# Moving VectorE's attention pieces, one lower half and one scaling in a fused attention and gated MLP kernel

## The chip, the cores and the metric

The kernel runs on one core of a Trainium2 chip. The metric is the device time in microseconds; lower is better. The kernel before takes 954.05 us (median of three runs, 953.96 to 954.59).

## What is computed

The reference is a linear attention without softmax, a root-mean-square norm over each head, and a two-layer MLP whose gate is h * erf(softplus(h)):

```python
kv = np.einsum('bhsd,bhse->bhde', k, v)
out = np.einsum('bhsd,bhde->bhse', q, kv)
rms = np.sqrt(np.mean(out * out, axis=-1, keepdims=True) + 1e-06)
x = (out / rms * g_norm)            # 8 batches, 8 heads, 576 rows, 64 columns
x = x.transpose(0, 2, 1, 3).reshape(4608, 512)
h = x @ w_in                        # 512 x 2048
sp = np.maximum(h, 0.0) + np.log1p(np.exp(-np.abs(h)))
return (h * erf(sp)) @ w_out        # 2048 x 512
```

The two weight matrices arrive in double precision, as pairs of 32-bit words; the rest is single precision.

## The kernel before

The 4608 rows are cut into nine groups T of 512 rows. Groups 0 to 7 hold 512 of the 576 rows of one batch each; group 8 collects the 64 rows left over ("tails") of all eight. The hidden width of 2048 is cut into 16 slices f of 128.

**Exact products from three forms.** From group 1 on, the products are made from rounded parts: a value x is split into an upper part (ScalarE, `upper`, L588), a lower part x - upper (VectorE, `lower_only`, L591) and a combination of both (VectorE, `both_only`, L594). One product (`product`, L642) is twelve matmuls of 512 columns: eight into `n_ps` (upper and lower forms) and four into `m_ps` (combined form). ScalarE scales `n_ps` out of PSUM (L1034, L899), VectorE adds `m_ps` (`add`, L628).

**Preparing the weights.** A 64-bit word pair becomes one single-precision number in `w_split` and `w_join`. `w_split` runs on ScalarE: it scales the upper word into `w_e` (L220) and converts the lower word into `w_m` (L221). `w_join` runs on VectorE: a shift (L230), the sign bit (L233) and an addition (L240). Eighteen pieces are converted, four of 512 columns and fourteen of 1024. `w_order` and `due` set when: `weights` splits one piece ahead of the one it joins. Four pieces are split in the prelude, the others in or after step 0. In step group 1 the weights are also split into their three forms, `w_upper` on ScalarE (L612) and `w_lower` on VectorE (L615, L618), and stored in DRAM, from which they are fetched again for each later group.

**Steps n = 0 to 31** handle groups 0 and 1, one slice f per step. A step makes h of one slice (L884, or `hidden` L650), its softplus, and the projection of the slice of five steps earlier (`project`, L706). Every four steps ScalarE applies Erf (L919). `steps[f]` holds three lists of attention pieces: the first is run at the step's start (behind up to two `w_lower`), the second behind the softplus, the third behind the projection. `pieces_of` fills them.

**Batches m = 8 to 36** handle groups 2 to 8 with four slices each (b = 0 to 3 in a group). A batch has four units i: a hidden product into PSUM, ScalarE's scaled copy, VectorE's add, ScalarE's softplus (L1049). Then ScalarE applies Erf (L1053), VectorE multiplies h by it (L1076) to give g, and four results j follow: the product of g's forms of the previous batch with `w_out`, each added into `e` by two VectorE instructions (L969 or L623, and L628). g of the previous batch is cut in two halves, `cut_upper` (ScalarE) in unit 0 and `cut_lower` (VectorE) for half 0 in unit 0 and for half 1 in unit 1. Results 0 and 1 read half 0, results 2 and 3 read half 1.

**The attention of the next group** is threaded through the batches, one pair p of heads per batch, as pieces run at `places`: 0, 2, 3, 5, 6 and 8 (the last batch of a group: 7). Place i + 1 is behind unit i, place 5 + j behind result j. In groups 3 to 7 the "visit" (L439) at place 2 makes, on TensorE, the attention output of pair p (L446, L454) and already the turned q and the kv product of the next pair (L466). Behind it ScalarE squares the output (L472), and `turned` copies the turned q (ScalarE, L338) and, for even pairs, the tails (VectorE, L345). At place 3 VectorE halves the square into two parts (`halve`, L500, L501), keeps the tail's output (`keep_tail`, L477) and reduces kv (`kv_kept`, L354, L361). Place 5 is the mean (L516, L517) with Ln, Exp and a square on ScalarE (L531 to L533), with activation tables loaded around them; place 6 is norm on VectorE (L539, L542, L551); place 8 cuts x into three forms. The next group's first hidden product needs those forms of all four pairs.

In groups 1 and 2 `prepare` (L366) makes the turned q and kv of its own pair, a step ahead of the visit, and calls `turned` and `kv_kept`.

**Queues.** Each engine works its instructions off in the order in which this code writes them; PSUM has six banks in rotation for the products (`banks`, three pairs) and one two-bank tile `at_ps` for the visit.

Of the kernel before, what the change touches and what calls it, by code (L numbers as in the profile page):

```python
# [39 lines left out]
FP32 = mybir.dt.float32  # L40
# [3 lines left out]
AF = mybir.ActivationFunctionType  # L44
ALU = mybir.AluOpType
# [5 lines left out]
BATCH = 4  # L51
# [3 lines left out]
FIRST = 2  # L55
# [5 lines left out]
def kernel(  # L61
# [10 lines left out]
    nc = tc.nc  # L72
# [6 lines left out]
    NP = H // 2  # L79
# [67 lines left out]
    def load_last(T, p):  # L147
        if T < B:
            nc.sync.dma_start(
                out=q_last[p % 2 * R : p % 2 * R + R, p // 2],  # L150
                in_=q[T, 2 * p : 2 * p + 2, G:S, :].rearrange("h r d -> r h d"),
            )

    g_col = const.tile([P, 1], FP32, name="g_col")
    for i in range(2):
        nc.gpsimd.dma_start(
            out=g_col[i * D : i * D + D, :], in_=g_norm.rearrange("(d one) -> d one", one=1)
# [29 lines left out]
    w_raw, w_cv = {}, {}  # L187
# [17 lines left out]
    def words(which, f):  # L205

        raw = w_raw[which, f]
        hi, lo = (
            raw.bitcast(kind).rearrange("p (n two) -> p n two", two=2)[:, :, half]
            for kind, half in ((FP32, 1), (U32, 0))  # L210
        )
        return hi, lo, raw.rearrange("p (n two) -> p n two", two=2)[:, :, 1]

    def w_split(which, f, k):


        hi, lo, _ = words(which, f)
        e = early.tile([P, G * k], I32, name="w_e", tag="w_e", bufs=2)
        m = early.tile([P, G * k], I32, name="w_m", tag="w_m", bufs=2)
        nc.scalar.activation(e.bitcast(FP32), hi, AF.Copy, scale=2.0**-112)  # L220
        nc.scalar.activation(m, lo, AF.Copy, scale=2.0**-29)  # L221
        w_cv[which, f] = e, m

    def w_join(which, f, k):


        hi = words(which, f)[2]
        e, m = w_cv.pop((which, f))
        w_raw.pop((which, f))
        nc.vector.tensor_scalar(  # L230
            out=e, in0=e, scalar1=3, scalar2=None, op0=ALU.logical_shift_left
        )
        nc.vector.scalar_tensor_tensor(  # L233
            out=e, in0=hi, scalar=-(1 << 31), in1=e, op0=ALU.bitwise_and, op1=ALU.bitwise_or
        )
        if which == "in":
            out_ = w_in_sb[:, f : f + k].rearrange("p t c f -> p (t c f)")
        else:
            out_ = w_out_sb[:, f : f + k, :].rearrange("p t f -> p (t f)")
        nc.vector.tensor_tensor(out=out_.bitcast(I32), in0=e, in1=m, op=ALU.add)  # L240
# [5 lines left out]
        + [(min(f + LAG, (f + FC) // 2 + 1), "out", f, 2) for f in range(0, FC, 2)]  # L246
    )
    w_at = {"load": 0, "split": 0, "join": 0}

    def w_next(what):  # L250
        i = w_at[what]
# [29 lines left out]
    def halves_of(t):  # L281
        return t.rearrange("p (a t) -> p a t", a=2)
# [50 lines left out]
    def turned(T, p, ps):  # L333

        qT = attp.tile([P, G], FP32, name="qT", tag="qT")
        if isinstance(ps, tuple):
            for a in range(2):
                nc.scalar.copy(halves_of(qT)[:, a], ps[a][:, 0 : 2 * P])  # L338
        else:
            nc.scalar.copy(halves_of(qT), ps[:, :, 0 : 2 * P])  # L340
        if p % 2 == 0:
            tails[T] = attp.tile([P, 2, R], FP32, name="qT_last", tag="t")
            for a in range(2):
                t = ps[a] if isinstance(ps, tuple) else ps[:, a]
                nc.vector.tensor_copy(out=tails[T][:, a], in_=t[:, 2 * P : 2 * P + R])  # L345
        if p == NP - 2:
            for i in range(NP):
                load_last(T + 1, i)
        ready[T, p] = qT, tails[T][:, p % 2]

    def kv_kept(T, p, at):

        kv = kv_of(T, p)
        nc.vector.tensor_reduce(  # L354
            out=kv[:, 0:D],
            in_=at[:, :, kv_cols].rearrange("p a e -> p e a"),
            op=ALU.add,
            axis=mybir.AxisListType.X,
        )
        for i in range(2):  # L360
            nc.vector.tensor_copy(out=kv[rows_of[1 - i], D : 2 * D], in_=kv[rows_of[i], 0:D])  # L361
# [4 lines left out]
    def prepare(T, p):  # L366

        at = at_tile()
        for product_ in turn_products(T, p, (at[:, 0], at[:, 1])):
            product_()  # L370
        for product_ in kv_products(T, p, at, crossed=False):
            product_()
        turned(T, p, at)
        kv_kept(T, p, at)

    def attention(T, p, pools=None):

# [5 lines left out]
        then = divmod(T * NP + p + 1, NP)  # L383
# [55 lines left out]
        def visit():  # L439


            qT, tail = ready.pop((T, p))
            at = st["at"] = at_tile()
            x = halves_of(qT)
            for a, i, o in ((0, 0, 0), (0, 1, 1), (1, 0, 1), (1, 1, 0)):
                nc.tensor.matmul(  # L446
                    at[rows_of[o], a, 0 : 2 * P],
                    lhsT=bd[rows_of[i], a * D : a * D + D],
                    rhs=x[rows_of[i], a],
                    start=True,  # L450
                    stop=True,
                )
            for s in rows_of:
                nc.tensor.matmul(  # L454
                    at[s, 0, 2 * P : 2 * P + R], lhsT=bd[s, 0:D], rhs=tail[s], start=True, stop=True
                )
            st["o"] = at[:, :, 0 : 2 * P]
            st["next"] = fused and then[0] < B
            if st["next"]:
                ps = pair_of_banks("q0_ps", "q1_ps")  # L460
                kvs = list(kv_products(*then, at, crossed=True))
                turns = list(turn_products(*then, ps))
                while kvs or turns:
                    for some in (turns, kvs):
                        for product_ in some[:4]:
                            product_()  # L466
                        del some[:4]
            if fused:
                st["sq"] = x_new.tile([P, G], FP32, name="sq", tag="x")
            else:  # L470
                st["sq"] = qT
            nc.scalar.activation(two(st["sq"]), st["o"], AF.Square)  # L472
            if st["next"]:
                turned(*then, ps)

        def keep_tail():
            nc.vector.tensor_copy(  # L477
# [96 lines left out]

        prepare_ = partial(prepare, T, p)
        if fused:
            first_ = (prepare_,) if (T, p) == (FIRST + 1, 0) else ()
            pieces = (first_, (visit,), (halve, keep_tail, loads))
        elif halves:
            pieces = ((prepare_,), (visit,), (halve, keep_tail, loads))  # L580
        else:
            pieces = ((prepare_, loads), (visit,), (keep_tail,))
# [187 lines left out]
            w_next(what)  # L770


    first_batch, batches = FIRST * NB, NG * NB
    w_seq = {
        which: [(which, f) for _ in range(NG - FIRST) for f in range(FC)] for which in ("in", "out")
# [15 lines left out]
    def pieces_of(T):  # L791


        steps = [([], [], []) for _ in range(FC)]
        for p in range(NP):
            products, apply, halve, mean, norm, split = attention(T, p)
            f = (BATCH - 1) * (p + 1) if T < FIRST else BATCH * p

            steps[f][2 if T == FIRST or p == 1 else 1].append(products)
            steps[f + 1][1].append(apply)  # L800
            steps[f + 2][0].append(halve)
            with_erf = (f + 2) % BATCH == BATCH - 1

            place = 2 if T < FIRST and p == 0 else 1
            steps[f + 2][place].append(partial(mean, table=not with_erf))
            steps[f + 3][0].append(norm)
            steps[min(f + 4, FC - 1)][0].append(split)
        return steps
# [27 lines left out]
    for n in range(FIRST * FC + 1):  # L836
        T, f = divmod(n, FC)
# [9 lines left out]
        if T < FIRST:  # L847
            if f == 0:
                steps = pieces_of(T + 1)
# [105 lines left out]
    def cut_lower(h, half, t):  # L955
        lower(part(h, half), *(t[:, i] for i in range(3)))
# [27 lines left out]
    for m in range(first_batch, batches + 1):  # L984
# [25 lines left out]
        def pieces(place):  # L1010
            while todo and places[-len(todo)] <= place:
                todo.pop(0)()
# [15 lines left out]
        for i in range(BATCH):  # L1028
            if m < batches:
                n_ps, m_ps = hidden(T, b * BATCH + i)  # L1030
            fetch(i)

            def evacuate():
                nc.scalar.activation(h[:, i], n_ps, AF.Copy, scale=SHIFT - 1.0)  # L1034
                add(h[:, i], m_ps)


            early_copy = i == 0 and m == B * NB
            if early_copy:
                evacuate()  # L1040
            if i == 0:
                for half in range(done, 2):
                    g.append(cut_upper(old_h, half))
            if done <= i < 2:
                cut_lower(old_h, i, g[i])
            if m < batches:
                if not early_copy:
                    evacuate()
                nc.scalar.activation(s[:, i], h[:, i], AF.Softplus)  # L1049
            pieces(i + 1)  # L1050
        if m < batches:
            for i in range(2):
# [29 lines left out]
        old_h = h  # L1082
# [33 lines left out]
```

## Time and profile before

| | us |
|---|---|
| device time, median of three | 954.05 |
| span of the profiled execution | 952.8 |
| TensorE busy (matmuls) | 924.1 |
| VectorE busy | 720.2 |
| ScalarE busy | 617.2 |
| first steady batch starts (hidden product of m = 8) | 255.8 |
| visits of group 5 (L446), starts | 564.25, 588.50, 612.90, 637.15 |
| norm of the same batches (L539), starts | 581.04, 606.15, 631.26, 656.36 |

In the profile's lines, DVE is VectorE, ACT is ScalarE, PE is TensorE's matmuls and PEld its weight loads. A timeline line gives the start in the execution, the duration, the engine, the line of the code, the instruction, what it writes and reads, how often, and in brackets the idle time of the engine just before it with what ended it. Matmuls are pipelined, so a matmul's listed duration is longer than the distance to the next one.

### The profile page before, as it was taken

How to read it: one execution, taken by the hardware profiler on the slowest of the kernel's cores; microseconds unless marked ns; L12 is line 12 of the kernel's file. 1: busy time of each engine (PE TensorE's matmuls, PEld its weight loads, DVE VectorE, ACT ScalarE, POOL GpSimd, SP SyncE). 2: the span in 40 equal slices, each digit the busy share in tenths (PEclk: the TensorE clock that was granted, in tenths of full speed). 3: DMA queues.
4: the chain of work that ended last, by engine and by line, in shares of the span. 5: the costliest groups of instructions: out<-in, count | busy, mean ns of one | idle time of the engine just before them, and what ended most of it. 6: DMA issues, size and time to landing. Idle time of an engine off the chain costs nothing.

```text
span 952.8 us, 15391 instructions
## 1 busy us (share of the span) xinstructions
PE 924.1 (97%) x5998; PEld 685.8 (72%) x5998; DVE 720.2 (76%) x1060; ACT 617.2 (65%) x844; POOL 2.4 (0%) x10
## 2 busy tenths in 40 slices
PE   6999999999999999999999999999999999999998
PEld 4444445656687877887788878886888788888886
DVE  2777648887677787888688878888787877788667
ACT  3999876776766666666656666666666666665552
POOL 1000000000000000000000000000000000000000
PEclk9999999999999999999999999999999999999999
DMA  9866406888789898899689978987887668777872
GB/s 255 290 191 207 140 1 232 320 351 313 233 304 338 327 336 303 298 340 322 203 285 327 312 268 315 325 300 252 271 320 260 256 240 346 283 272 300 346 272 61
DMA packets 108271, 259.99 MB, mean 273 GB/s; under 512 B 43992, under 2 KB 66856, under 8 KB 108200
## 3 DMA queue, kind: packets, MB, share of 16 engines
q1 hardware_dynamic: 106488, 256.73, 76.2%
q10 hardware_dynamic: 1648, 2.29, 0.8%
q8 instruction: 47, 0.77, 0.3%
q14 instruction: 24, 0.20, 0.1%
q0 software_dynamic: 64, 0.00, 0.0%
HBM read 224.40 MB, written 34.60 MB: 272 GB/s over the span
## 4 chain that ended last, share of the span: by engine, by line
PE 65%; DVE 15%; ACT 11%; DMA 4%; issue 3%; SPq 0%; DVEq 0%; ACTq 0%
PE n_ps L650 31%; PE m_ps L650 16%; PE o_ps L706 9%; PE h_ps L884 4%; DVE h L628 3%; ACT s L1053 2%; DVE g_forms L591 2%; DVE e L628 2%; DMA w_raw<-in_moe_w_in_dram 1%; ACT L105 1%; ACT L1053 1%; DMA w_in_parts<-w_in 1%; PE at_ps L446 1%; DVE x L551 1%; DVE u L542 1%
## 5 line engine op out<-in xcount | busy, mean ns | idle before, releaser
L650 PE MATMUL n_ps<-x_forms,w_in_parts 128*128 128x512 f32 x896 | 229.8, 397 | 9.0 <-DVE x_forms L591 4.2
L650 PE MATMUL n_ps<-w_out_parts,g_forms 128*128 128x512 f32 x928 | 232.5, 392 | 0.9 <-DVE qT_last L345 0.9
L1049 ACT ACTIVATE s<-h 128x512 f32<-128x512 f32 x112 | 70.8, 633 | 209.7 <-DVE h L628 209.7
L650 PEld LDWEIGHTS n_ps<-x_forms,w_in_parts 128*128 128x128 f32 x896 | 168.2, 190 | 49.1 <-ACT x_forms L588 6.0
L650 PEld LDWEIGHTS n_ps<-w_out_parts,g_forms 128*128 128x128 f32 x928 | 172.5, 188 | 39.3 <-DVE qT_last L345 2.2
L650 PE MATMUL m_ps<-w_out_parts,g_forms 128*128 128x512 f32 (+1 forms) x468 | 124.3, 388 | 0.0
L650 PE MATMUL m_ps<-x_forms,w_in_parts 128*128 128x512 f32 x448 | 120.8, 392 | 0.0
L628 DVE TENSOR_TENSOR h<-m_ps,h 128x512 f32<-128x512 f32 x116 | 79.7, 687 | 52.4 <-ACT h L1034 34.9
L706 PE MATMUL o_ps<-w_out_sb,h_sb 128*128 128x512 f32 x224 | 101.7, 597 | 0.2 <-DVE h_sb L834 0.2
L650 PEld LDWEIGHTS m_ps<-w_out_parts,g_forms 128*128 128x128 f32 x468 | 87.5, 188 | 18.4
L650 PEld LDWEIGHTS m_ps<-x_forms,w_in_parts 128*128 128x128 f32 x448 | 84.5, 189 | 17.8
L628 DVE TENSOR_TENSOR e<-m_ps,e 128x512 f32<-128x512 f32 (+1 forms) x117 | 80.3, 687 | 16.7 <-PE m_ps L650 8.4
L623 DVE SCALAR_TENSOR_TENSOR e<-n_ps,e 128x512 f32<-128x512 f32 x88 | 60.2, 684 | 22.7 <-PE n_ps L650 22.7
L706 PEld LDWEIGHTS o_ps<-w_out_sb,h_sb 128*128 128x128 f32 x224 | 41.4, 190 | 44.7 <-issue 42.1
L594 DVE SCALAR_TENSOR_TENSOR g_forms<-g_forms 128x1024 fp32r<-128x1024 f32 x58 | 71.0, 1225 | 2.0
L591 DVE TENSOR_TENSOR g_forms<-h,g_forms 128x1024 fp32r<-128x1024 f32 x58 | 70.5, 1216 | 0.7 <-ACT g_forms L588 0.7
L1034 ACT ACTIVATE h<-n_ps 128x512 f32<-128x512 f32 x112 | 66.0, 590 | 4.5 <-PE n_ps L650 4.4
L1076 DVE TENSOR_TENSOR h<-h,s 128x1024 f32<-128x1024 f32 x56 | 65.9, 1218 | 0.7 <-ACT s L1053 0.7
L884 PE MATMUL h_ps<-xT,w_in_sb 128*128 128x512 f32 x144 | 64.8, 596 | 1.7 <-DVE w_in_sb L240 1.7
L588 ACT ACTIVATE g_forms<-h 128x1024 fp32r<-128x1024 f32 x58 | 58.5, 1048 | 12.2 <-PE m_ps L650 8.7
L108 ACT ACT_TABLE_LOAD x44 | 56.5, 1283 | 0.7
L1053 ACT ACTIVATE s<-s 128x1024 f32<-128x1024 f32 x56 | 56.3, 1052 | 0.3
(127 smaller groups left out, 1030.9 us busy)
## 6 DMA issues: line engine op xcount, KB each, us to landing
w_out_parts<-w_out SPq DMA_DIRECT2D x116, 768.0 KB
w_in_parts<-w_in SPq DMA_DIRECT2D x112, 768.0 KB
w_in<-w_new SPq DMA_DIRECT2D x16, 768.0 KB
q_sb<-in_q_dram SPq DMA_DIRECT2D x32, 256.0 KB
w_raw<-in_moe_w_in_dram SPq DMA_DIRECT2D x16, 512.0 KB
w_raw<-in_moe_w_out_dram SPq DMA_DIRECT2D x8, 1024.0 KB
out_dram<-e SPq DMA_DIRECT2D x32, 256.0 KB
k_sb<-in_k_dram SPq DMA_DIRECT2D x28, 287.5 KB
```

Of the source, the lines that this page charges most:

```text
L588: nc.scalar.activation(high, x, AF.Copy, scale=1.0 + 2.0**-13)
L591: nc.vector.tensor_tensor(out=low, in0=x, in1=high.bitcast(FP32), op=ALU.subtract)
L594: nc.vector.scalar_tensor_tensor(out=both, in0=low.bitcast(FP32), scalar=SHIFT, in1=high.bitcast(FP32), op0=ALU.mult, op1=ALU.add,)
L623: nc.vector.scalar_tensor_tensor(out=out_, in0=ps, scalar=scale, in1=out_, op0=ALU.mult, op1=ALU.add)
L628: nc.vector.tensor_tensor(out=out_, in0=ps, in1=out_, op=ALU.add)
L650: nc.tensor.matmul(ps[:, cols], lhsT=weights(form, k), rhs=moving(form, k)[:, cols], start=(form == forms[0] and k == 0), stop=(form == fo ...
L706: nc.tensor.matmul(o_ps[j], lhsT=g[:, j * P : j * P + P], rhs=w_out_sb[:, f, :], start=(f == 0), stop=last,)
L884: nc.tensor.matmul(plain[i], lhsT=w_in_sb[:, i % FC, c], rhs=xT[T][:, c, :], start=(c == 0), stop=(c == KC - 1),)
L1034: nc.scalar.activation(h[:, i], n_ps, AF.Copy, scale=SHIFT - 1.0)
L1049: nc.scalar.activation(s[:, i], h[:, i], AF.Softplus)
L1053: nc.scalar.activation(part(s, i), part(s, i), AF.Erf)
L1076: nc.vector.tensor_tensor(out=part(h, half), in0=part(h, half), in1=part(s, half), op=ALU.mult)
```

## The change

Three things are changed. (1) In groups 3 to 7, `halve` and `keep_tail` (with `kv_kept`) move from place 3 to place 2, directly behind the visit; the loads stay at place 3. Where `prepare` is used, the tails' copies and `kv_kept` are split off as `keep_prepared` and run at the start of the next step. (2) `cut_lower` of g's half 1 moves from unit 1, ahead of that unit's add, to unit 3, behind that unit's softplus. (3) From step 0 on, the upper word's scaling is no longer a ScalarE instruction of `w_split` but a VectorE multiplication at the head of `w_join`. The purpose is to have VectorE's short attention pieces done while VectorE would otherwise wait, to bring unit 1's add forward, and to take work off ScalarE in the first steps.

```diff
     def w_split(which, f, k):
-        nc.scalar.activation(e.bitcast(FP32), hi, AF.Copy, scale=2.0**-112)
+        if not w_late:
+            nc.scalar.activation(e.bitcast(FP32), hi, AF.Copy, scale=2.0**-112)
...
     def w_join(which, f, k):
+        if late_:
+            nc.vector.tensor_scalar(
+                out=e.bitcast(FP32), in0=scaled, scalar1=2.0**-112, scalar2=None, op0=ALU.mult
+            )
...
-        turned(T, p, at)
-        kv_kept(T, p, at)
+        qT = turned(T, p, at)
+        def keep():
+            tails_kept(T, p, at, qT)
+            kv_kept(T, p, at)
+        kept.append(keep)
...
-            pieces = (first_, (visit,), (halve, keep_tail, loads))
+            first_ = (prepare_, keep_prepared) if (T, p) == (FIRST + 1, 0) else ()
+            pieces = (first_, (visit, halve, keep_tail), (loads,))
...
+    w_late.append(True)
     first_batch, batches = FIRST * NB, NG * NB
...
             steps[f][2 if T == FIRST or p == 1 else 1].append(products)
+            steps[f + 1][0].append(keep_prepared)
             steps[f + 1][1].append(apply)
...
-            if done <= i < 2:
-                cut_lower(old_h, i, g[i])
+            if i == 0 and not done:
+                cut_lower(old_h, 0, g[0])
             if m < batches:
...
                 nc.scalar.activation(s[:, i], h[:, i], AF.Softplus)
+            if i == BATCH - 1:
+                cut_lower(old_h, 1, g[1])
             pieces(i + 1)
```

## The prediction

> **What bounds the kernel now.** I read the engine totals, the waits, the timelines of VectorE, ScalarE and TensorE, and the spaces between matmul starts. Totals: TensorE 924.1 of 952.8 us, VectorE 720.2, ScalarE 617.2. TensorE looks full, yet it still stands still now and then. Timeline of TensorE where group 4 ends and group 5 begins (start, duration, instruction, idle before it):
>
> ```profile
> 556.41 1.52 PE L650 MATMUL n_ps<-x_forms,w_in_parts 128*128 128x512 f32 x6
> 558.86 0.50 PE L650 MATMUL n_ps<-x_forms,w_in_parts 128*128 128x512 f32 x1 [0.93 <-ACT x_forms L588]
> 560.20 0.50 PE L650 MATMUL n_ps<-x_forms,w_in_parts 128*128 128x512 f32 x1 [0.83 <-DVE x_forms L591]
> ```
>
> It waits for the attention result of the new group. From start to start of matmuls (0.226 us each when unhindered) such a gap costs 1.8 to 2.2 us, once in each of groups 2 to 6 (a group here is the one whose MLP batches run). Between gaps TensorE's visits (L446) come every 24.26, 24.40, 24.25 us. But norm (L539, first instruction) starts at 505.74, 530.84, 555.94, 581.04, 606.15: every 25.10. So VectorE and ScalarE fall 0.8 us behind per batch and TensorE pays at the group's end. What closes that 25.10? Timeline of VectorE, then of ScalarE, for one batch:
>
> ```profile
> 505.74 0.69 DVE L539 SCALAR_TENSOR_TENSOR u<-at_ps,u 128x512 f32<-128x512 f32 x1 [0.61 <-ACT u L533]
> ...
> 514.36 0.68 DVE L628 TENSOR_TENSOR h<-m_ps,h 128x512 f32<-128x512 f32 x1
> 514.97 1.21 DVE L591 TENSOR_TENSOR g_forms<-h,g_forms 128x1024 fp32r<-128x1024 f32 x1
> 516.21 1.23 DVE L594 SCALAR_TENSOR_TENSOR g_forms<-g_forms 128x1024 fp32r<-128x1024 f32 x1
> 517.36 0.68 DVE L628 TENSOR_TENSOR h<-m_ps,h 128x512 f32<-128x512 f32 x1
> 520.26 0.69 DVE L628 TENSOR_TENSOR h<-m_ps,h 128x512 f32<-128x512 f32 x1 [2.22 <-ACT h L1034]
> 520.87 0.42 DVE L500 CAST sq_hi<-sq 128x512 fp32r<-128x512 f32 x1
> ...
> 522.80 0.69 DVE L628 TENSOR_TENSOR h<-m_ps,h 128x512 f32<-128x512 f32 x1
> ...
> 530.84 0.69 DVE L539 SCALAR_TENSOR_TENSOR u<-at_ps,u 128x512 f32<-128x512 f32 x1 [1.45 <-ACT u L533]
> ```
>
> ```profile
> 518.07 0.63 ACT L1049 ACTIVATE s<-h 128x512 f32<-128x512 f32 x1 [1.88 <-DVE h L628]
> 518.61 0.58 ACT L472 ACTIVATE sq<-at_ps 128x512 f32<-128x512 f32 x1
> 519.09 0.64 ACT L338 COPY qT<-q_ps 128x256 f32<-128x256 f32 x2
> 519.60 0.62 ACT L1034 ACTIVATE h<-n_ps 128x512 f32<-128x512 f32 x1
> ...
> 523.52 0.63 ACT L1049 ACTIVATE s<-h 128x512 f32<-128x512 f32 x1 [1.42 <-DVE h L628]
> ```
>
> Read as one chain: norm 505.74, VectorE without a pause to the add of unit 1 at 517.36 (the g cut at 514.97 lies in it), softplus, square, two turn copies and copy of unit 2 on ScalarE, add of unit 2 at 520.26, the halving pieces, add of unit 3 at 522.80, softplus 523.52, Erf, Ln, Exp, square, norm 530.84. No link waits for TensorE: it is a VectorE-ScalarE loop, 25.10 us long.
>
> [...] matmuls are pipelined; the trace agrees (392 ns each, 226 ns apart), hence the starts. [...] the tail copy (L345) of 494.38 starts as the first turn copy (493.99, mean 375 ns) ends. [...]
>
> **Part 1: VectorE's pieces behind the visit, g's second lower half two units on.** These act together. Take norm as 0. Add of unit 0 stays at 8.62 (514.36-505.74). The cut (2.39, from 514.97 to 517.36) goes away behind it. Then ScalarE sets the pace by the spacings above: softplus 9.33, copy of unit 1 9.87, add of unit 1 10.53, softplus 11.24, square 11.78 (12.87 before), turn copies 12.26, copy of unit 2 12.77. VectorE's new wait is that for the square: queued behind it are the adds of units 2 and 3, for which ScalarE's softplus waits. It ends at 12.39; cast 0.45, rest 0.61, x_last 0.13, reduction 0.31, copies 0.43 = 1.93. Add of unit 2: 14.32 (14.52 before). Softplus, copy, add of unit 3: +0.72+0.54+0.66 = 16.24 (17.06 before).
> From there two ways lead to the next norm. ScalarE: 0.72 + (530.84-523.52) = 8.04, so 24.28. VectorE: 0.61, the moved cut 2.39, four result adds 2.78, the gate product 2.27: 8.05, so 24.29. Thus the cut fills the idle time that VectorE had between result 0 and norm (0.63+0.23+1.45 at 525.5, 526.4 and 530.8) entirely.
> In batches 1 and 3 of a group two tail copies stand ahead of the halving and wait for the turn copies: the cast starts at square + 1.28 (by 493.51 and 494.38 to 494.65 for the copies, 0.14 for the last) = 13.06 rather than 12.39. These batches take 24.29+0.67 = 24.96.
> Batch 0 after a gap is limited by TensorE: visit 8.31 after norm (564.25-555.94), next norm 16.38 after the visit (277.92-261.55, 480.64-464.26): 24.69. Where the interval of half TensorE clock falls there (459.8 to 463.2 and 661.2 to 664.6, by the granted clock of these stretches) it is 26.34 before and after.
> A group is thus 24.69+24.96+24.29+24.96 = 98.90 instead of 100.40. Sum of savings: group 2, two batches, 0.81+0.14 = 0.95 (the first two are bound by TensorE and one DMA wait); groups 3 and 5, 1.50 each; group 4, 1.09; group 6, 1.26 (its last batch has no next pair: 23.57 for 23.88). Total 6.3. TensorE has room for it: its own time per group, 4 x 24.3 = 97.3, stays below. Its small waits for tails and x_last inside groups (0.58, 0.21, 0.61, 0.63) vanish, at no gain, as it waits at the boundary anyway.
> Does the later cut make TensorE wait? g's second half is first needed low at result 2, begun 20.1 after norm (550.97-530.84); the low form is ready at 16.91+0.61+1.22 = 18.74. Free by 1.4. Result 3 needs result 0's banks, free at 21.4, begun at 22.9. Nothing. The loads keep their place; q_last's are issued ahead of the tail copies, but wait only for TensorE's turns: nothing.
> Group 7 and the tail group run TensorE without gaps (22.66 per batch), so they keep what was won and add nothing.
>
> **Part 2: the shift on VectorE.** 14 of 18 conversions drop a ScalarE instruction of 1151 ns and gain a VectorE one over 1024 elements at stride 2. Lower bound 0.69 (L230, contiguous, 689 ns), upper 1.22 (L233, 1225 ns). [...] I take 0.69. TensorE runs this stage without pauses except:
>
> ```profile
> 57.34 3.70 PE L884 MATMUL h_ps<-xT,w_in_sb 128*128 128x512 f32 x8 [1.72 <-DVE w_in_sb L240]
> ```
>
> 1.89 by starts. The join ending at 57.28 follows x_last (53.95), which follows the square (53.34), behind two removed scalings on a full ScalarE. Reworked in order the square starts at 50.9, x_last 51.55, multiplication and join 0.73+3.2: 55.6 (56.1 with 1.22). TensorE arrives at 55.4 to 55.6: saving 1.7 (1.2). Elsewhere 14 x 0.7 = 10 us lie in VectorE's idle time (2 to 4.7 us stretches at 63.8 to 131) with joins 2 us or more early.
>
> **Part 3: the kept tails and kv one step later.** In step group 1 the deferred piece comes after two weight cuts (w_lower, 2.66) in VectorE's queue. At attention pairs 0, 2 and 3 VectorE was waiting for the turn copy, so the cuts fill idle time, and the mean's two waits for x_last (0.76 at 154.8, 1.01 at 211.4) go. At pair 1 it was not waiting. VectorE's timeline, then TensorE's:
>
> ```profile
> 173.84 1.28 DVE L739 COPY e<-o_ps 128x512 f32<-128x512 f32 x2
> 175.04 0.28 DVE L354 TENSOR_REDUCE bd_kv<-at_ps 128x64 f32<-128x128 f32 x1
> 175.35 0.39 DVE L361 COPY bd_kv<-bd_kv 64x64 f32<-64x64 f32 x2
> 175.78 0.69 DVE L615 SCALAR_TENSOR_TENSOR w_new<-w_new,w_out_sb 128x512 fp32r<-128x512 f32 x1
> ```
>
> ```profile
> 176.53 0.66 PE L446 MATMUL at_ps<-qT,bd_kv 64*64 64x256 f32 x8
> ```
>
> With the cuts first, bd_kv is done at 175.04+2.66+0.74 = 178.44; the visit needs it, and TensorE's queue behind (project, the next unit) waits 1.9. Net of part 3: -0.76-1.01+1.92 = +0.15.
>
> **Sum.** -6.3-1.7+0.15 = -7.85; 954.05-7.85 = 946.2.
>
> **Rivals.** A, the loop keeps 25.10 because each shortened link meets a hidden handover of about 0.8 (the trace shows none, but the VectorE way has under 0.1 of room over ScalarE's): only parts 2 and 3 count, 954.05-1.55 = 952.5. B, slower: VectorE's queue stalls at the halving until ScalarE's copy of unit 2 is done (13.39 instead of 12.39), holding the adds behind it: 25.29, and 25.96 with tails, mean 25.6, +0.5 over 18 batches = +9; less 1.55: 961.5. Against it: in step group 1 the cast (236.33) followed the square (235.72, 0.58) at once. C, pair 1's wait does not arise: 944.3.
>
> **How the numbers follow.** My case 0.66 (946.2), C 0.12, A 0.14, B 0.08. Part 1 is uncertain by about 2, part 2 by 1.2, part 3 by 1.9: 943.5 to 950.5 leaves out about 2 in 10, A and B. Faster: my case, C and about half of A, 0.86; same 0.07; slower 0.07.
>
> **What would show it.** Norm starts 24.3 and 25.0 us apart in turn; gaps at the groups' ends still 1.3 to 1.8 us; e's first result add straight behind the moved cut; the multiplication 0.69 us; TensorE at 57 going on 1.2 to 1.7 us earlier; a new wait of about 1.9 us for bd_kv near 176. Wrong: norm still at 25.1, or TensorE waiting for g_forms at result 2.

## The result, and the profile after

The changed kernel takes 943.59 us (median of four runs, 943.36 to 945.18); the kernel before 954.32 us (median of four, 953.96 to 957.49). The ratio is 0.9884, interval 0.986 to 0.9908: faster, as forecast, but by 10.7 us and not the 7.85 of the likeliest case. The 943.59 us lie at the very edge of the forecast range (943.5 to 950.5); by the ratio, from the 954.05 us on which that range was built, they are 943.0, just below it. The experiments below ask two things: does the loop work as the prediction's chain says, and where do the 3 us come from?

**The loop.** VectorE's timeline of the changed kernel over one batch with tail copies, from one norm (L560) to the next (columns as before: start, duration, engine, line, instruction, what it writes and reads, idle time ahead of it):

```profile
476.93 0.68 DVE L560 SCALAR_TENSOR_TENSOR u<-at_ps,u 128x512 f32<-128x512 f32 x1
...
485.55 0.68 DVE L649 TENSOR_TENSOR h<-m_ps,h 128x512 f32<-128x512 f32 x1
487.41 0.69 DVE L649 TENSOR_TENSOR h<-m_ps,h 128x512 f32<-128x512 f32 x1 [1.18 <-ACT h L1057]
489.54 0.50 DVE L358 COPY qT_last<-q_ps 128x64 f32<-128x64 f32 x2 [1.44 <-ACT qT L344]
489.96 0.42 DVE L521 CAST sq_hi<-sq 128x512 fp32r<-128x512 f32 x1
...
491.90 0.69 DVE L649 TENSOR_TENSOR h<-m_ps,h 128x512 f32<-128x512 f32 x1
493.77 0.69 DVE L649 TENSOR_TENSOR h<-m_ps,h 128x512 f32<-128x512 f32 x1 [1.18 <-ACT h L1057]
494.38 1.22 DVE L612 TENSOR_TENSOR g_forms<-h,g_forms 128x1024 fp32r<-128x1024 f32 x1
...
496.77 0.68 DVE L992 TENSOR_SCALAR e<-n_ps 128x512 f32<-128x512 f32 x1
...
501.83 0.68 DVE L560 SCALAR_TENSOR_TENSOR u<-at_ps,u 128x512 f32<-128x512 f32 x1
```

Counted from norm: add of unit 1 at 10.48, cast of the square at 13.03, adds of units 2 and 3 at 14.97 and 16.84, next norm at 24.90. The working had 10.53, 13.06, 14.99, 16.91 and 24.96 for such a batch. The moved cut (494.38) stands where it was expected, the first result add straight behind it, and VectorE doesn't pause from 493.77 to the next norm. ScalarE's timeline shows the other half of the loop:

```profile
488.13 0.63 ACT L1072 ACTIVATE s<-h 128x512 f32<-128x512 f32 x1 [0.76 <-DVE h L649]
488.67 0.58 ACT L492 ACTIVATE sq<-at_ps 128x512 f32<-128x512 f32 x1
489.15 0.64 ACT L344 COPY qT<-q_ps 128x256 f32<-128x256 f32 x2
489.66 0.62 ACT L1057 ACTIVATE h<-n_ps 128x512 f32<-128x512 f32 x1
492.62 0.63 ACT L1072 ACTIVATE s<-h 128x512 f32<-128x512 f32 x1 [2.34 <-DVE h L649]
```

The square starts 11.74 after norm, 1.1 earlier than before; but ScalarE then stands still for 2.34 us, because unit 2's add now queues behind the tail copies and the halving on VectorE.

**The ends of the groups.** TensorE's timeline of the changed kernel where group 4's batches begin:

```profile
453.60 2.02 PE L671 MATMUL n_ps<-x_forms,w_in_parts 128*128 128x512 f32 x7
456.44 0.50 PE L671 MATMUL n_ps<-x_forms,w_in_parts 128*128 128x512 f32 x1 [0.82 <-DVE x_forms L612]
...
457.73 2.00 PE L671 MATMUL n_ps<-x_forms,w_in_parts 128*128 128x512 f32 x8
459.56 0.62 PE L671 MATMUL m_ps<-x_forms,w_in_parts 128*128 128x512 f32 x2
```

One wait of 0.82 is left; before there were two here, 0.99 and 0.84. Look also at the next unit: its eight matmuls go from 457.73 to 459.56, 1.83 us (0.23 from start to start, though the single one at 456.44 is listed with 0.50). In the kernel before the same eight went from 459.90 to 463.25, 3.35 us:

```profile
459.90 3.51 PE L650 MATMUL n_ps<-x_forms,w_in_parts 128*128 128x512 f32 x8
463.25 1.08 PE L650 MATMUL m_ps<-x_forms,w_in_parts 128*128 128x512 f32 x4
```

The busy times by windows show why. Columns: window, its length, busy time (and instructions) of TensorE, its weight loads, VectorE, ScalarE and GpSimd, then the granted TensorE clock, the DMA engines' share and GB/s. Kernel before:

```profile
456.35:459.75 3.40, 1.69 (x6) 1.19 (x7) 3.26 (x6) 3.13 (x4) 0.00 (x0) 1.00 0.37 154
459.76:463.17 3.41, 3.41 (x10) 2.65 (x9) 3.27 (x5) 0.00 (x0) 0.00 (x0) 0.50 0.50 184
```

Changed kernel, at the same place in the work:

```profile
452.00:455.40 3.40, 3.40 (x15) 2.44 (x13) 3.23 (x6) 2.41 (x4) 0.00 (x0) 1.00 0.78 283
455.41:458.80 3.39, 2.57 (x11) 1.95 (x11) 3.25 (x6) 2.15 (x3) 0.00 (x0) 1.00 0.38 149
```

Before, a stretch in which TensorE was busy for only half the time (1.69 of 3.40 us) is followed by 3.41 us at half clock. After, TensorE is busy for three quarters (2.57 of 3.39) and no half clock follows, here or at the start of group 6. A clock row of 24 us slices, as the profile's overview gives it, shows a 9 (90% or more) in every slice for both kernels: it is too coarse for this.

**Waits of the first steps, and a DMA.** TensorE's timeline of the changed kernel at the conversion near 55, at attention pair 1, and in batch 9:

```profile
55.72 2.84 PE L907 MATMUL h_ps<-xT,w_in_sb 128*128 128x512 f32 x6 [0.55 <-DVE w_in_sb L245]
...
175.48 0.86 PE L466 MATMUL at_ps<-qT,bd_kv 64*64 64x256 f32 x6 [1.63 <-DVE bd_kv L364]
...
290.84 3.14 PE L671 MATMUL n_ps<-x_forms,w_in_parts 128*128 128x512 f32 x8 [1.93 <-DMA w_in_parts<-w_in]
```

By matmul starts, as in the prediction: 0.71 lost near 55 (1.89 before), 1.80 at pair 1 (new), 2.09 at the DMA wait in batch 9 (1.06 before). This execution pays for that last wait a second time, as the windows show:

```profile
288.15:291.56 3.41, 1.48 (x7) 0.96 (x6) 2.87 (x9) 1.11 (x4) 0.00 (x0) 1.00 1.01 419
291.57:294.98 3.41, 3.41 (x9) 2.65 (x8) 0.00 (x0) 1.23 (x2) 0.00 (x0) 0.50 1.06 407
```

The DMA engines are full here (share 1.01), so what TensorE gained before it partly waits again. The profiled execution is the one of 945.18 us, mean clock 0.998; the three of 943.36 to 943.66 us had 1.000.

**The ledger.** Between landmarks of the two profiled executions (visits of the attention on TensorE, norms on VectorE), in us:

| stretch | before | after | difference |
|---|---|---|---|
| start to first visit | 46.93 | 46.48 | -0.45 |
| first to second visit (the wait near 55) | 22.32 | 21.14 | -1.18 |
| second visit to visit of m = 8 (kept tails and kv) | 192.30 | 191.92 | -0.38 |
| that visit to norm of m = 9 (DMA wait, here with half clock) | 42.18 | 44.81 | +2.63 |
| norm of m = 9 to norm of m = 27 (the loop) | 453.03 | 442.98 | -10.05 |
| norm of m = 27 to the end | 196.1 | 196.1 | 0.0 |

The sum is -9.4, as the spans say (952.8 and 943.4). The loop's share was forecast as -6.3, so this row holds the time that the forecast lacked.

### The profile page after: what moved, and what is told of

Its sections match the earlier page's. It is cut to its first block, busy times and chain, and to the rows that moved or that the text cites. A ratio compares the mean times of both kernels' runs of the same rounds, so it can differ in the third digit from the quotient of the medians.

```text
span 943.4 us, 15388 instructions
## 1 busy us (share of the span) xinstructions
PE 920.1 (98%) x5998; PEld 685.3 (73%) x5998; DVE 728.8 (77%) x1074; ACT 603.1 (64%) x830; POOL 2.4 (0%) x10
## 4 chain that ended last, share of the span: by engine, by line
PE 71%; DVE 16%; ACT 6%; DMA 4%; issue 2%; SPq 0%; DVEq 0%; ACTq 0%
PE n_ps L671 35%; PE m_ps L671 17%; PE o_ps L727 8%; PE h_ps L907 4%; DVE e L649 3%; DVE h L1101 2%; DVE e L644 2%; DVE h L649 2%; PE at_ps L466 1%; DVE g_forms L612 1%; DMA w_in_parts<-w_in 1%; PE at_ps L486 1%; DMA k_sb<-in_k_dram 1%; DVE x L572 1%; DVE u L563 1%
## 5 line engine op out<-in xcount | busy, mean ns | idle before, releaser
L1057 ACT ACTIVATE h<-n_ps 128x512 f32<-128x512 f32 x112 | 66.1, 590 | 10.4 <-PE n_ps L671 10.2
```

## The experiments

The theory behind the prediction (T) says that the recurrence above (the times of a batch, worked out link by link from the norm before it) sets the loop. For the missing time there are two candidates: the half clock is brought about by TensorE's gap at the group's end, so that shortening the gap removed it; or it comes by chance or at fixed times, and the loop itself gained more than worked out. Times in this part are medians; each ratio is to the kernel before, run alongside (954.58 to 955.09 us). The changed kernel ran at another time; where a run is set against it, the difference by the two ratios is given too.

### Both moves of the batches together

```diff
-            pieces = (first_, (visit,), (halve, keep_tail, loads))
+            pieces = (first_, (visit, halve, keep_tail), (loads,))
...
-            if done <= i < 2:
-                cut_lower(old_h, i, g[i])
+            if i == 0 and not done:
+                cut_lower(old_h, 0, g[0])
...
+            if i == BATCH - 1:
+                cut_lower(old_h, 1, g[1])
```

> The kernel before with both moves in the batches (halving directly behind the visit, g's second lower half at unit 3), no other part of the change. Theory T (the working of the prediction, with one correction: the intervals of half TensorE clock are caused by the TensorE gap at a group's end and vanish when the gap is short): norm starts 24.2, 24.9, 24.7, 24.9 us apart in a group, no half-clock interval at the groups' ends, 954.1 - 6.3 - 3.3 = 944.5 us. Rival F (half-clock intervals come at fixed times or at random, whatever the gaps): two of them stay, 947.8 us.

Measured: 944.39 us, ratio 0.9893 (0.9876 to 0.9909). Norms are 24.7, 24.9, 24.25 and 24.9 apart in each group, and there is no half clock in the whole stretch. The time is T's 944.5, not F's 947.8. So nearly all of the gain is in the batches, and the loop explains the interval lengths, with the half clock gone.

### The later cut alone

The second half of the diff above.

> The kernel before with only g's second lower half moved from unit 1 to unit 3; the halving stays at place 3. By the same recurrence: norm = 0, add of unit 1 at 10.53, square 11.78, copy of unit 2 12.77, add of unit 2 at 13.43 (it no longer stands behind the halving), halving from 14.04, add of unit 3 at 15.97, next norm 15.97 + 8.05 = 24.02 in batches with and without tails. That is below TensorE's own 24.3, so TensorE becomes the bound and the gaps at the groups' ends nearly close. Theory T: faster than the whole change by 2 to 4 us, near 940 to 942 us, no half-clock interval. Rival R (the early halving is what shortens the loop): slower than the whole change, 948 us or more.

Measured: 939.25 us, ratio 0.9843 (0.9822 to 0.9865). One part of the change alone beats the whole by 4.3 us (3.9 by the ratios), and is a little faster than T's 940 to 942. Norms are now 24.40, 24.26, 24.40 and 24.69 apart, and the first three are TensorE's own visit spacing: the loop has dropped below TensorE. VectorE's timeline of this kernel:

```profile
498.19 0.69 DVE L539 SCALAR_TENSOR_TENSOR u<-at_ps,u 128x512 f32<-128x512 f32 x1
...
511.59 0.69 DVE L628 TENSOR_TENSOR h<-m_ps,h 128x512 f32<-128x512 f32 x1 [2.22 <-ACT h L1034]
512.20 0.42 DVE L500 CAST sq_hi<-sq 128x512 fp32r<-128x512 f32 x1
...
514.13 0.69 DVE L628 TENSOR_TENSOR h<-m_ps,h 128x512 f32<-128x512 f32 x1
514.74 1.22 DVE L591 TENSOR_TENSOR g_forms<-h,g_forms 128x1024 fp32r<-128x1024 f32 x1
...
522.46 0.68 DVE L539 SCALAR_TENSOR_TENSOR u<-at_ps,u 128x512 f32<-128x512 f32 x1
```

Here unit 2's add is at 13.40 after norm and unit 3's at 15.94; in the changed kernel they come at 14.97 and 16.84 in a batch with tails. The halving behind unit 2's add lies in the time in which ScalarE makes softplus and copy anyway. And TensorE at the same group's start no longer waits:

```profile
451.47 2.38 PE L650 MATMUL n_ps<-x_forms,w_in_parts 128*128 128x512 f32 x8
453.69 1.09 PE L650 MATMUL m_ps<-x_forms,w_in_parts 128*128 128x512 f32 x4
```

Eight starts take 2.22 us, 0.4 more than unhindered, in place of a gap of 1.1.

### The early halving alone

The first two lines of the diff above.

> The kernel before with only the halving, the tail and kv moved directly behind the visit. By the recurrence of theory T: add of unit 1 stays at 11.62 after norm, square 12.87, halving 13.48 to 15.41, add of unit 2 at 15.4 instead of 14.5, add of unit 3 at 17.3, next norm 25.4, with tails 26.0; over 18 batches about +0.6 each: 961 to 966 us, with half-clock intervals still there. Rival R: a shorter loop, faster than 952 us.

Measured: 965.96 us, ratio 1.0118 (1.0097 to 1.0139): slower. Norms 26.01 apart with tail copies and 25.35 without, where the recurrence gave 26.04 and 25.37. The gaps at the groups' ends grow to 3.1 us and half clock follows at three of them in this execution. VectorE's timeline shows the cause, in a batch with the cut still in unit 1 and no tails:

```profile
524.01 0.68 DVE L628 TENSOR_TENSOR h<-m_ps,h 128x512 f32<-128x512 f32 x1
525.88 0.43 DVE L500 CAST sq_hi<-sq 128x512 fp32r<-128x512 f32 x1 [1.19 <-ACT sq L472]
...
527.83 0.69 DVE L628 TENSOR_TENSOR h<-m_ps,h 128x512 f32<-128x512 f32 x1
529.70 0.69 DVE L628 TENSOR_TENSOR h<-m_ps,h 128x512 f32<-128x512 f32 x1 [1.19 <-ACT h L1034]
```

VectorE waits 1.19 for the square, whose start the cut has put off, and then has 1.9 us of pieces to do ahead of the add for which ScalarE's softplus waits. Of the two moves, the cut gains and the halving costs.

### The changed kernel with the halving put back

```diff
-            pieces = (first_, (visit, halve, keep_tail), (loads,))
+            pieces = (first_, (visit,), (halve, keep_tail, loads))
```

> The whole change with only the halving, the tail and kv put back to place 3. Theory T: as the moved cut and the scaling, plus the new wait for bd_kv at pair 1 (1.8) less the two waits for x_last that it takes away (0.76, 1.01): within 0.5 us of the kernel with cut and scaling alone, 937 to 938.5. If the later keeping costs by itself, 939 or more.

Measured: 938.72 us, ratio 0.9837 (0.9822 to 0.9852), 4.9 us under the changed kernel's median (4.5 by the ratios) and between the two forecasts; norms 24.40, 24.26, 24.40 and 24.7 apart as with the cut alone. This is the same finding from the other side.

### The scaling on VectorE alone, and with the cut

The hunks of `w_split`, `w_join` and `w_late`, alone (first) and on top of the later cut (second).

> The kernel before with only the upper word's scaling moved to VectorE from step 0 on. Both theories: the wait of TensorE for w_in_sb near 57 us falls from 1.9 to 0.7 us, everything after it comes 1.2 to 2 us earlier, the batches are unchanged at 25.10: 952 to 953 us. Theory T adds that the half-clock intervals may move to other groups, as the gaps come to lie otherwise against the 3.41 us raster on which the intervals begin: each one more or less is 1.7 us. Rival F: they stay near 459.8 and 661.2.

> The kernel before with g's second lower half moved and the upper word's scaling on VectorE, without the early halving and without the later keeping of tails and kv in step groups 0 and 1. Theory T: cut_only (939.3) less the 1.2 to 2 us of the scaling: 937.3 to 938.1, below the whole change by 5 to 6. Rival R (the other two parts of the change are needed): not below the whole change's 943.6.

Measured: 953.67 us, ratio 0.9987 (0.9973 to 1.0), barely clear of no difference, and 939.43 us, ratio 0.9851 (0.9834 to 0.9867), the same as the cut alone. In the first kernel's profile norms are still 25.1 apart, and half clock stands at 559.8 and 662.2, so it did move to another group, as T allowed. The multiplication, which the prediction could only bound, is in the groups by form:

```profile
L232 DVE TENSOR_SCALAR w_e<-w_raw 128x1024 f32<-128x1024 f32 x14 | 9.6, 688 | 0.1
```

688 ns: the lower bound, which the prediction took as its author's estimate, was right. First to second visit takes 20.74 us in both kernels, 1.6 less than the 22.32 before. But TensorE's wait in batch 9 is 1.46 and 1.64 instead of 1.06 and 0.99 (in the first of these two the profile names ScalarE's turn copy as what came last, in the other three the DMA). So a quarter to two fifths of the gain seems to be taken back there, and the rest is within what varies between executions (the cut alone had 21.40 to the second visit with no scaling moved). The second run missed its expectation by 1.3 us; the longer wait would account for half of that, and the other half isn't settled. The other traces agree on the wait: with the scaling on VectorE (seven traces) it is 1.37 to 2.09, without it (six, leaving out the one shifted in time) 0.66 to 1.06.

### Kept tails and kv one step later, alone, and pair 1 put back

The first kernel is the kernel before with `keep_prepared` and its call. The second is the changed kernel with:

```diff
-            steps[f + 1][0].append(keep_prepared)
+            if T == FIRST and p == 1:
+                steps[f][2].append(keep_prepared)
+            else:
+                steps[f + 1][0].append(keep_prepared)
```

> The kernel before with part 3 alone: tails and kv kept one step later in groups 1 and 2. Theory: one new wait of 1.8 us for bd_kv at pair 1 of step group 1, two waits for x_last (0.76 and 1.01) gone: +0.1, so 954 to 955 with the half-clock intervals of the kernel before; norm 25.10 apart as before. Rival: the two waits for x_last are only moved to the DMA wait in batch 9, and +1.8 is left: 956.

> The changed kernel with one thing put back: in step group 1, pair 1's tails and kv are kept at the end of their own step again. Theory: TensorE's wait of 1.8 us for bd_kv near 174 goes and nothing takes its place: 941.8. Rival: the next steps have slack, TensorE arrives earlier at the DMA wait in batch 9 and waits there that much longer: 943.5, as the changed kernel.

Measured: 955.31 us, ratio 1.0001 (0.9991 to 1.0011), no difference; and 941.53 us, ratio 0.9863 (0.9833 to 0.9894), 2.1 us under the changed kernel's median (2.0 by the ratios; three of its four runs lie within 0.3 us, the fourth is at 945.25, and its interval takes in the changed kernel's ratio). TensorE's timeline of the second at pair 1 has no wait any more:

```profile
173.16 1.09 PE L671 MATMUL m_ps<-x_both,w_new 128*128 128x512 f32 x4
174.18 0.66 PE L466 MATMUL at_ps<-qT,bd_kv 64*64 64x256 f32 x8
```

From the second visit to that of m = 8 the first takes 192.34 (before 192.30), the second 190.45. So part 3 as a whole is worth nothing because one place gives back what two others gain, and the one place can be left as it was. The wait in batch 9 is 1.37 in the second kernel's profile, not longer than the 2.09 of the changed kernel: its rival isn't borne out here.

### Filling TensorE's gap

The kernel before, with matmuls into `m_ps` that are overwritten afterwards, put in front of the two waiting matmuls of each group's first hidden product (groups 3 to 7).

```diff
+                    if fill and k == 3 and ps is n_ps:
+                        for _ in range(fill):
+                            nc.tensor.matmul(
+                                m_ps, lhsT=weights(0, 0), rhs=moving(0, 0), start=True, stop=True
+                            )
                     nc.tensor.matmul(
...
+                fill = 4 if FIRST < T < NG - 1 and b == 0 and i == 0 else 0
-                n_ps, m_ps = hidden(T, b * BATCH + i)
+                n_ps, m_ps = hidden(T, b * BATCH + i, fill=fill)
```

> The kernel before; in the first hidden product of groups 3 to 7 TensorE issues, before each of the two matmuls that wait for the new group's x forms, four more matmuls (0.9 us) into the bank that the combined product overwrites afterwards. They add work, but only in TensorE's idle time; the VectorE-ScalarE loop is untouched. Theory T (the idle share of a 3.41 us raster interval sets off the half clock): idle at these gaps falls from 2.2 to about 0.5 us, no half-clock interval at the groups' ends any more, 954.1 - 3.3 = 950.8 us, norm 25.10 apart throughout. Rival F (intervals of half clock independent of the gaps): 954 us or a little more, with intervals at half clock.

Measured: 952.09 us, ratio 0.9972 (0.9962 to 0.9983), all runs between 951.33 and 953.22, 2.7 us under the kernel before (954.82), where T had 3.3. The kernel does 40 matmuls more and takes less time. Norms are 25.11 apart throughout groups 3 to 6: the loop isn't touched, and the two intervals of 26.3 are gone. TensorE's timeline, with the added matmuls in the gap (L652):

```profile
453.78 1.52 PE L655 MATMUL n_ps<-x_forms,w_in_parts 128*128 128x512 f32 x6
455.14 1.07 PE L652 MATMUL m_ps<-x_forms,w_in_parts 128*128 128x512 f32 x4
456.23 0.50 PE L655 MATMUL n_ps<-x_forms,w_in_parts 128*128 128x512 f32 x1
456.57 1.10 PE L652 MATMUL m_ps<-x_forms,w_in_parts 128*128 128x512 f32 x4
457.56 0.50 PE L655 MATMUL n_ps<-x_forms,w_in_parts 128*128 128x512 f32 x1
```

### Shifting the work in time

The kernel before with such matmuls once, in the first unit of batch 8. `fill` is 8 here, and these eight are put in front of each of two matmuls: sixteen, 3.6 us of work, where the expectation reckoned with eight and 1.8 us. TensorE's timeline:

```profile
257.83 1.98 PE L652 MATMUL m_ps<-x_forms,w_in_parts 128*128 128x512 f32 x8
...
259.87 1.98 PE L652 MATMUL m_ps<-x_forms,w_in_parts 128*128 128x512 f32 x8
```

> The kernel before; eight matmuls (1.8 us) more in TensorE's first steady product (m = 8), which is bound by TensorE, so that everything behind comes 1.8 us later, the gaps as long as before. Theory T: the gaps then lie otherwise against the raster: that of group 3 (358 to 360.3) falls into one raster interval, those of groups 4 and 6 straddle two, so half clock is seen behind other gaps than 459.8 and 661.2; total 955.9 us plus or minus 1.7 per interval more or fewer. Rival F: half clock at 459.8 and 661.2 as before, 955.9 us.

Measured: 957.4 us, ratio 1.0033 (1.002 to 1.0046), 2.6 us more than the kernel before: the 3.6 less the DMA wait of 1.06 in batch 9, which no longer arises in this trace. The half clock is now at 462.1 and 564.5, at the starts of groups 4 and 5, not of 4 and 6. It isn't tied to a time of the span. Which gap it would follow was guessed wrong: the shift was twice the one reckoned with, and, as shown below, the grid on which the half clock begins doesn't start at the same time in each trace (14.96 to 20.49 us into the span).

### Making the gap long again

The changed kernel with VectorE held back at the end of norm of a group's last pair:

```diff
+            if FIRST < T < B and p == NP - 1:
+                for _ in range(3):
+                    nc.vector.tensor_scalar(
+                        out=x, in0=x, scalar1=1.0, scalar2=None, op0=ALU.mult
+                    )
```

> The changed kernel with VectorE held back by three in-place multiplications of x by 1.0 (0.42 us each by the nearest row, 1.27 in all, values unchanged) between norm and the cut into forms of pair 3 in groups 3 to 7, so that TensorE's gap at the end of groups 2 to 6 grows from 1.1-1.4 to about 2.4 us. Theory (half TensorE clock follows a gap of about 2 us or more): 5 x 1.2 = 6 us of longer gaps, partly taken back by the next batch's start, and one to four intervals of half clock of 1.7 us each are back in the hidden product after such a gap: 950 to 956. Rival (half clock has nothing to do with these gaps, the missing intervals were chance): no interval of half clock behind these gaps, 949 to 950.

Measured: 954.67 us (951.97 to 959.73), ratio 1.0003 (0.9992 to 1.0015): 1.35 us put in at each of five places cost 11 us and make the change worth nothing. TensorE's timeline and then the windows of this kernel:

```profile
456.65 0.51 PE L676 MATMUL n_ps<-x_forms,w_in_parts 128*128 128x512 f32 x1 [1.43 <-ACT x_forms L614]
457.99 0.51 PE L676 MATMUL n_ps<-x_forms,w_in_parts 128*128 128x512 f32 x1 [0.83 <-DVE x_forms L617]
```

```profile
455.47:458.88 3.41, 1.40 (x5) 0.94 (x6) 3.24 (x7) 2.88 (x4) 0.00 (x0) 1.00 0.35 146
458.88:462.30 3.42, 3.42 (x10) 2.67 (x9) 3.28 (x4) 0.25 (x1) 0.00 (x0) 0.50 0.40 102
```

Half clock is back after two of the five gaps (458.9 and 660.3), where 2.39 and 2.78 us of idle time fall into one window. Norms into a new group are 26.1 apart, 1.4 more than in the changed kernel, and 27.7 with half clock. 5 x 1.4 and 2 x 1.6 make 10.2 of the 11. The rival (no half clock, 949 to 950) falls.

### Halving and pair 1 both put back

The changed kernel with the two diffs above that put a part back.

> The changed kernel with halving and kept tails back at place 3 in groups 3 to 7 (the later cut of g and the scaling on VectorE stay) and pair 1's tails and kv kept in their own step. Theory: 938.7 (measured with the first alone) less the 1.8 us wait: 937. Rival: the DMA wait in batch 9 grows by what the wait at pair 1 gives up: 938.5.

Measured: 938.32 us (936.72 to 940.06), ratio 0.9817 (0.9783 to 0.9851). That is the lowest median, but it can't be told from the 938.72 without the second diff. TensorE arrives earlier in batch 9 and waits longer there (timeline, then windows):

```profile
289.55 2.63 PE L671 MATMUL n_ps<-x_forms,w_in_parts 128*128 128x512 f32 x8 [1.87 <-DMA w_in_parts<-w_in]
```

```profile
287.44:290.84 3.40, 1.53 (x8) 1.11 (x7) 2.88 (x9) 1.44 (x4) 0.00 (x0) 1.00 1.00 413
290.85:294.25 3.40, 3.40 (x10) 2.63 (x9) 0.26 (x1) 0.60 (x1) 0.00 (x0) 0.50 1.08 413
```

By starts the wait is 2.03, and in this execution half clock follows it. The rival, which has the DMA take back what pair 1 gives up, has 938.5 and is closer to the median than the theory's 937; four runs over 3.3 us don't decide between them.

## Why the prediction was right and where it was wrong

**The bound.** Right. The intervals follow the recurrence, not TensorE, for the change (24.23 and 24.89 against 24.29 and 24.96; the first batch of a group has 24.7 against 24.69 and is TensorE's, as forecast), for the halving alone, and for the cut alone, where it falls below TensorE and TensorE's spacing takes over. Rival A (a hidden handover keeps 25.10) and rival B (the queue stalls at the halving, 25.3 to 26.0) did not come about. The halving without the cut has about B's numbers (25.35 and 26.01), but not B's mechanism: there the cast starts as the square ends (525.88), without waiting for ScalarE's copy of unit 2, and the square itself is late because the cut stands ahead of it.

**Part 1.** The chain was right to 0.1 us at each link, and so were the tails: 24.89 - 24.23 = 0.66 for a forecast 0.67 (VectorE's copy at 489.54 waits 1.44 for ScalarE's turn copy). What wasn't asked is what each of the two moves does by itself: taken apart, the later cut gives 15.8 us and the early halving takes 4 to 5 of them back. (TensorE's own time per group is 4 x 24.3 = 97.2, not 97.3; nothing hangs on it.)

**The step that failed.** "Where the interval of half TensorE clock falls there (459.8 to 463.2 and 661.2 to 664.6, by the granted clock of these stretches) it is 26.34 before and after." The two intervals measured 24.72 and 24.67. That is 1.62 + 1.67 = 3.29 us. The other sixteen intervals of the loop are on average 0.03 us shorter than worked out, 0.46 together: -6.3 - 3.29 - 0.46 = -10.05, the ledger's row. The half clock was taken as part of the machine's time, but it was a consequence of the very gap that the change shortens. The prediction had the gap's length after the change (1.3 to 1.8 us, measured 1.1 to 1.4) beside the two intervals, and did not connect them. Filling the gap removed them with the loop left alone (-2.7 us); lengthening the gap brought two of them back.

**Part 2.** 1.7 was forecast; from the first to the second visit 1.2 came in the profiled execution (which also reached the first visit 0.45 earlier, so the second came 1.63 earlier) and 1.6 in most others with the scaling. But the step "at no gain" was not applied to the DMA wait of batch 9, which the prediction named only as a bound of the first two batches. It grew from 1.06 to 2.09 in the changed kernel. The forecast also put the rest of the first steps at nothing; with the scaling alone, second visit to visit of m = 8 takes 191.96, 0.34 less than before.

**Part 3.** Right: a new wait of 1.80 (forecast 1.92), two waits for x_last gone, +0.04 on the landmark for a forecast +0.15. Rival C (no wait at pair 1) did not come about.

**The sum.** In the profiled pair: -7.85, with -3.29 for the half clock, -0.46 for the intervals, +0.1 for the start with part 2 (-1.63 for -1.7), -0.5 for the stretch of part 3 (-0.38 for +0.15) and +2.6 for batch 9 (1.0 of DMA wait and 1.6 of half clock), makes -9.4, the ledger's sum. Without that half clock, which by their clock of 1.000 the three faster runs did not have, it would be -11.0; the medians differ by -10.7.

## What to carry to other kernels

A gap of TensorE can cost more than its length: where a stretch of half clock stands behind a gap in the trace, it may be that gap's doing. Here fourteen of fifteen came behind 2.03 us or more of idle time in one window, and the two of the loop cost 1.62 and 1.67 us; an estimate of what a shorter gap is worth has to allow for it. When a change moves two pieces at once, work the recurrence out for each alone, since one may pay for the other, as the cut did here for the halving. And time won ahead of a stretch with full DMA engines (share 1.01 here, where the wait grew from 1.06 to 2.09 us) isn't won until that stretch's own wait has been worked out anew.

## What the runs showed of the hardware

**The half clock followed a window, not a gap.** In the fourteen traces there are fifteen windows of half clock inside the work. They lie on a grid: in the kernel before the two begin 661.14 - 459.76 = 201.38 us apart, which is 59 times 3.413 us (one lasts 3.41), and all fifteen begin a whole number of 3.413 us after the first full clock that their trace records: (459.76 - 16.02) / 3.413 = 130.0 and (661.14 - 16.02) / 3.413 = 189.0 in the kernel before, 81.0 after, 129.0 and 188.0 with the gap made long. If one cuts each trace into such windows and adds up TensorE's idle time in them (distances between matmul starts beyond the unhindered one, where they exceed it by over 0.1 us), fourteen of the fifteen come behind a window with 2.03 us of idle time or more, and no window with 1.97 or less has one behind it. (The fifteenth, in the halving alone, follows directly on another half-clock window, in which idle time can't be counted this way. The boundary at 2 us is not known closer than about 0.1: one window of the halving alone, with no half clock behind it, would come to 2.04 if a distance that is 0.104 too long were counted in.)

| kernel | idle in the window ahead of half clock | longest idle without half clock |
|---|---|---|
| before | 2.09, 2.32 | 1.51 |
| after | 2.08 | 1.80 |
| halving alone | 2.07, 3.06, 3.15 | 1.97 |
| scaling alone | 2.20, 2.25 | 1.59 |
| shifted in time | 2.15, 2.25 | 1.89 |
| kept tails alone | 2.17 | 1.83 |
| gap made long | 2.39, 2.78 | 1.76 |
| both put back | 2.03 | 1.40 |
| gap filled | none | 1.42 |
| the five others | none | 1.80 |

Such a window lasted 3.41 us and cost about 1.6 (1.62 and 1.67 in the two intervals above). A gap of 2.2 us that straddled two windows had no such effect (at 558.9 in the kernel before a gap of 2.2 leaves no more than 1.3 in one window), which is why the same gaps were hit in some groups and not in others. A window that was idle for three fifths (2.03 of 3.41 us) was enough. The grid doesn't start at a fixed time of the span: the first full clock is recorded at 16.02 us in the kernel before and at 15.09 in the changed one, and between 14.96 and 20.49 over all traces. That the same gap can fall differently from one execution of a kernel to the next is the author's estimate from this. It would explain why runs of the kernel before spread from 952.3 to 957.5 us while those of the gap filled stay within 951.3 to 953.2. The mean granted clocks of all runs fit: the 65 runs of the kernel before beside the experiments have 0.993 to 0.999, and their mean time rises from 952.8 us at 0.999 to 956.6 at 0.994; the eight with the gap filled all have 0.999 or 1.000, and the twenty with the gap made long have 0.990 to 0.997, where the changed kernel has 0.998 to 1.000. Where the windows of half clock lay in the runs without a trace isn't known.
